# x rows loaded in other pieces, and a rank for each instruction in place of one for each stage

## The chip, the cores and the metric

The kernel runs on one core of a Trainium2 chip. A core has five engines with a queue of their own each: TensorE (PE) for matmuls, ScalarE (ACT), VectorE (DVE), GpSimd (POOL) and SyncE (SP, which here only issues DMAs). The metric is device time of one execution in microseconds; lower is better. The kernel before takes 227.81 us (median of three runs, 227.30 to 228.36).

## The reference

Two branches over a sequence of S = 2048 rows of D = 640, bf16, mixed by a gate that is computed from the same input:

```python
x = A_q
g = sigmoid((x * gate_w).sum(-1, keepdims=True))
a = A(x, A_k, A_v, A_shift_k, A_ssm_k, A_ssm_D)
b = B(x, B_w1, B_w2, B_w3, B_w4)
return g * a + (1 - g) * b
```

`A`: k is convolved with four taps per channel (`shift_k`) and multiplied by v, which gives `kv`; `kv` is convolved along the whole sequence with `ssm_k` (by FFT in the reference), `kv * ssm_D` is added, and the sum is multiplied by q (= x). `B`: layernorm of x, `@ w1`, gelu, the four column groups shifted by +1, -1, +2, -2 rows, `@ w2`, plus x; then layernorm, `@ w3` (to 1536), gelu, `@ w4`, plus the residual.

## The kernel before

**Tiling.** Sequence row s = 1024 c + 8 p + r lies on partition p; c is 0 or 1 and r, "row r" below, 0 to 7. So x is 16 tiles of 128x640, two halves (c) for each row r.

**The order is planned at build time.** The kernel's text creates 924 nodes (one instruction or a short run of matmuls each) with their tiles, a rough cost and a tag such as `xn:4`. `Prog._forward` then walks a model of the core: again and again it takes, over all engines, the node that can start earliest, and where several can start at the same time, the one with the highest priority. That fixes the order of every engine's queue, the PSUM pair (one of four) of every matmul job, and, in `assign_waits`, the semaphore waits. On the chip each engine then works through its list in that order; an instruction at the head of a list that waits holds all that stands behind it. `PRIO` gives one priority for each tag, so all nodes of a tag share it. The model's rate for plain loads is `RATE`, and `land` is what it adds from a load's last byte to its landing.

**The stages, by tag.**
- `x` loads (L709): pieces of rows as `X_LOADS` says, each piece as two DMAs (c = 0, 1); row 0 goes out on ACT's queue, all other pieces on SP's. The other loads follow on SP: `w1`, `k`, `v`, `kh` (the halo rows of k), `w2`, `FM` (transform tables), `ssm`, `D`, `gw`, `shk`.
- `fill`: 96 short matmuls on ones (L744) that need nothing; the planner puts them where TensorE would have nothing else, and drops those behind the last real matmul.
- First layernorm by `LN1_GROUPS` = (0), (1), (2,3), (4,5), (6,7): statistics on VectorE (`bn`, two for each half of a row and one aggregation, L874 and L876), for row 1 on ScalarE (`st`); an inverse root on GpSimd (`ln`, L854); the normalised row on VectorE (`xn`, L654); ten transposes (`xTp`, L913) and their eviction (`xTe`).
- `mm1` (L953, with `gelu1`), `tail` (GpSimd DMAs that shift the last columns), `gate` (L1010, four jobs of twenty one-column matmuls), `mm2` (L1061; `seed2` puts the residual into PSUM before, L1043; `x1` evicts, `sq` squares), second layernorm, `xT` (transposing DMAs), `mm3` (L1115, with `gelu3`), `mm4` (L1133, with `B`).
- `kv`, `kvb`: the four taps and the product with v, all on VectorE (L649), in four quarters `:0` to `:3`.
- The long convolution, for the two halves of the columns (half 0 and 1): transforms of the taps (`fwdh`) and of kv (`fwdk`), both L1164, evicted by ScalarE (`Sh`, `Sk`, L680); a unit for each half and parity, `:0` to `:3`, on VectorE: butterflies (`bh`, `bk`), `win`, `pw` with one accumulating DMA `pwa` on GpSimd's queue (L688), `pwz`, `fold`; the inverse transform `inv` (L1352; the last four rows `invl`, L1327), its eviction with the gate (`gy`, `gyl`), the product with q and the sum (`fin`, `finl`; in half 0 the sum is an accumulating DMA `fina`, L1378), the store `out`, `outl`.

`fwdk` needs all four quarters of kv. The inverse of half 0 needs units 0 and 1, that of half 1 units 2 and 3.

The nodes are numbered as they are created; the numbers are the same before and after the change.

Of the kernel before, what the change touches and what calls it, by code (L numbers as in the profile page):

```python
# [88 lines left out]
class Prog:  # L89
# [86 lines left out]
        node.land = land or (1.1 if final else 2.2)  # L176
        return node

    PRIO = {}

    def schedule(self):
        for n in self.nodes:
            n.base = frozenset(n.deps)
        for j in self.jobs:
            own = set(j.nodes)
            j.ext = [d for v in j.nodes if not v.first for d in v.base if d not in own]
            if j.seeded:
                j.nodes[0].soft = [d for v in j.pes for d in v.base if d not in own]
        for n in self.nodes:
            for d in n.deps:  # L190
                d.users.append(n)
        for n in self.nodes:
            n.prio = self.PRIO.get(n.tag, 0.0)
        self._forward()

    RATE = 400e3
    WINDOW = 3.4133
    PHASE = 2.4

    def _forward(self):  # L200
# [38 lines left out]
        while left:  # L239
# [59 lines left out]
            elif n.kind == "dma":  # L299
                link = max(link, xlink, t + 1.2) + n.bytes / self.RATE  # L300
                n.end = link + n.land
# [125 lines left out]
def _bf16_bits(a):  # L427
# [7 lines left out]
KV_DMA = ()  # L435
PW1 = (0, 1, 2, 3)
PW2 = ()
X_LOADS = ((0, 1), (1, 2), (2, 4), (4, 6), (6, 8))
LN1_GROUPS = ((0,), (1,), (2, 3), (4, 5), (6, 7))
SPLIT = (0,)  # L440
LN2_DVE = ()
# [7 lines left out]
XQ = {(0, 0): "act", (0, 1): "act"}  # L449
# [2 lines left out]
FIN1_DMA = 0  # L452
SEED2 = (0, 1, 2, 3, 4, 5, 6, 7)
SEED4 = (0, 1, 2, 3, 4, 5, 6, 7)
PRIO = {
# [36 lines left out]
}  # L492


def _freq(kap):
# [41 lines left out]
def bass_gated_mix__ssm_conv_h3__mixer_s_mlp__prompt_kernel(  # L537
    nc, A_q, A_k, A_v, A_shift_k, A_ssm_k, A_ssm_D, B_x, B_w1, B_w2, B_w3, B_w4, gate_w, out,
):
    D, F = 640, 1536  # L540
    P = Prog(nc)
# [17 lines left out]
    def V(o, n):  # L559
        return AR[:, o:o + n]  # L560
# [25 lines left out]
    X = V(oX, 10240).rearrange("p (c r d) -> p c r d", c=2, r=8)  # L586
# [3 lines left out]
    w1v = V(oW12, 3200).rearrange("p (c f) -> p c f", c=5)  # L590
    w1t = V(oW12 + 3200, 640).rearrange("p (c f) -> p c f", c=5)
# [6 lines left out]
    GM = V(oGM, 4096).rearrange("p (a i r s k) -> p a i r s k", a=2, i=2, r=4, s=2)  # L598
# [9 lines left out]
    ident = V(oID, 128)  # L608
# [82 lines left out]
    def load(queue, o, i, nbytes, tag="", **kw):  # L691
        return P.dma(queue, lambda e, ps: e.dma_start(o, i), w=[o], nbytes=nbytes, tag=tag, **kw)  # L692

    def dram(ap, offset, dims):
        return bass.AP(tensor=ap.tensor, offset=ap.offset + offset, ap=dims)

    def rows(t, c):
        return t[0, 1024 * c:1024 * c + 1024, :].rearrange("(p r) d -> p r d", r=8)
# [6 lines left out]

    for a, b in X_LOADS:
        P.stage = a
        for c in range(2):
            load(XQ.get((a, c), "sp"), X[:, c, a:b, :], rows(A_q, c)[:, a:b, :], 163840 * (b - a), tag="x", land=1.4 if b < 3 else 2.2)  # L709
    P.stage = ""  # L710
    load("pool", V(oID, 256).bitcast(U16), cI.ap(), 65536, tag="ident", cost=0.6)
    load("sp", w1v, B_w1.rearrange("(c p) f -> p c f", p=128), 890000, tag="w1")
    load("sp", SHKROW, dram(A_shift_k, 0, [[2560, 1], [1, 2560]]), 5120, tag="shk")
    w1s, w1d = w1v.rearrange("p c (g f) -> p c g f", g=4)[:, :, :, 128:160], w1t.rearrange("p c (g f) -> p c g f", g=4)
    P.op("pool", lambda e, ps: e.tensor_copy(w1d, w1s), r=[w1s], w=[w1d], cost=1.2, tag="w1t")
# [90 lines left out]
    for c in range(3):  # L806
        P.stage = c
        n = 128 if c < 2 else 64
# [6 lines left out]
              tag="tap")  # L815
# [13 lines left out]
    for a in range(2):  # L829
        P.stage = a  # L830
        o = TAP[:, 1, 8 * a:8 * a + 8, :]
        for d in (0, 128, 256):
            n = min(128, 320 - d)
# [131 lines left out]
    for sc in range(4):  # L965
# [10 lines left out]
        for j, d0 in enumerate(SHIFT):  # L976
# [4 lines left out]
            for carry, lst in todo.items():  # L981
                k0, rho0, n = lst[0][0], lst[0][1], len(lst)
# [21 lines left out]
    for g in range(4):  # L1004
        P.stage = g
        fns = []
        for i in range(4):
            rho, c = 2 * g + i // 2, i % 2
# [37 lines left out]
    for g in range(4):  # L1046
        P.stage = g
        for i in range(4):
            rho, c = 2 * g + i // 2, i % 2
# [3 lines left out]
            for hh in range(2):  # L1053
                for ft in range(5):
                    if ft < 4:
                        q = rho - SHIFT[ft]
# [27 lines left out]
        for rho in rhos:  # L1084
            for c in range(2):
                b = normal(rho, c, mean[:, rho, c:c + 1], RS2, NB2 if g in LN2_ACT else None)
# [21 lines left out]
    for sc in range(4):  # L1108
# [14 lines left out]
        for i in range(4):  # L1123
            rho, c = 2 * sc + i // 2, i % 2
# [275 lines left out]
    q1 = load_q(1, "s3")  # L1400
    inverse(1, "k0", "t1", q1, "s0")

    P.PRIO = PRIO
    P.schedule()
    P.assign_waits()
    with nc.Block() as block:  # L1406
# [29 lines left out]
```

## Time and profile before

| | us |
|---|---|
| median of three runs | 227.81 (227.30 to 228.36) |
| the profiled execution, its own time | 227.51 |
| its span, first to last instruction | 225.7 |
| DMA traffic | 34.05 MB |

| engine | busy us | share of the span |
|---|---|---|
| TensorE, matmuls | 217.8 | 97% |
| TensorE, weight loads | 139.0 | 62% |
| VectorE | 208.1 | 92% |
| ScalarE | 174.8 | 77% |
| GpSimd | 42.6 | 19% |

The granted TensorE clock is 1.00 throughout. How to read the views below: a row of the chain of waits, or of the timeline, has its start, its length, the engine and the line; "[0.48 <-DMA x]" says that the engine stood idle for 0.48 us before it and that a DMA of x ended that. "SPq" is SP issuing a DMA. Matmuls are pipelined, so the length of a single one (299 ns for 320 columns) is not its price; a run of them, divided by their number, is.

### The profile page before, as it was taken

Reading aid. Unit: us, or ns where it says so; the run is one execution under the profiler, and the core shown is the slowest. Engines: PE = TensorE matmul, PEld = TensorE weight load, DVE = VectorE, ACT = ScalarE, POOL = GpSimd, SP = SyncE. Lnnn points to the kernel's source line nnn. Section 1 sums busy time; section 2 is a strip of 40 time slices with the busy share of each in tenths; the row PEclk is TensorE's granted clock in tenths of the full one; section 3 lists DMA queues with packets and bytes.
Section 4 is the critical chain, followed back from the end, with each engine's and each line's share of the span. In section 5 each row is a group of like instructions: output and inputs, shape, how many; then the busy total and the mean of one; then the engine's idle time right before and its main releaser. Section 6 shows DMA issues by size and latency. Waiting matters only on the chain.

```text
span 225.7 us, 3992 instructions
## 1 busy us (share of the span) xinstructions
PE 217.8 (97%) x1575; PEld 139.0 (62%) x1587; DVE 208.1 (92%) x267; ACT 174.8 (77%) x292; POOL 42.6 (19%) x48
## 2 busy tenths in 40 slices
PE   6999999999999999999999999999999999999992
PEld 6695855557776664457754467754465566577771
DVE  4899999999999969999999999649999999999985
ACT  5889979879999999999785885594593465574392
POOL 1143654460004220203203200000010000332010
PEclk9999999999999999999999999999999999999999
DMA  6999997779823948061441680000077018488576
GB/s 166 392 401 402 334 348 251 151 143 243 281 96 84 310 85 341 7 116 33 87 86 30 108 130 0 3 0 0 0 132 219 0 35 200 58 174 110 126 135 215
DMA packets 36714, 34.05 MB, mean 151 GB/s; under 512 B 17508, under 2 KB 31719, under 8 KB 36568
## 3 DMA queue, kind: packets, MB, share of 16 engines
q1 hardware_dynamic: 31560, 23.97, 36.7%
q0 software_dynamic: 4848, 9.50, 19.2%
q10 hardware_dynamic: 288, 0.33, 0.5%
q8 instruction: 12, 0.20, 0.4%
q14 instruction: 6, 0.05, 0.1%
HBM read 21.47 MB, written 3.93 MB: 113 GB/s over the span
## 4 chain that ended last, share of the span: by engine, by line
PE 60%; DVE 24%; DMA 5%; issue 4%; ACT 4%; SPq 2%; DVEq 0%
PE PS L1133 23%; PE PS L1115 23%; DVE arena L649 20%; PE PS L1164 8%; PE PS L1352 6%; DMA arena<-in_A_q_dram 5%; ACT arena L680 3%; SPq L692 2%; DVE arena L874 2%; DVE arena L654 1%; PE PS L1061 1%; DVE arena L876 0%; ACT PS L1043 0%; DVE arena L1337 0%; DVEq L1406 0%
## 5 line engine op out<-in xcount | busy, mean ns | idle before, releaser
L649 DVE TENSOR_TENSOR arena<-arena 128x2560 bf16<-128x2560 bf16 (+5 forms) x175 | 185.9, 1120 | 10.4 <-ACT arena L680 8.9
L680 ACT ACTIVATE arena<-PS 128x640 bf16<-128x640 f32 (+6 forms) x142 | 104.9, 821 | 20.2 <-PE PS L1115 14.9
L1133 PE MATMUL PS<-arena 128*128 128x320 bf16 x384 | 54.0, 299 | 0.0
L1115 PE MATMUL PS<-arena 128*128 128x512 bf16 x232 | 51.4, 379 | 0.6 <-issue 0.2
L1133 PEld LDWEIGHTS PS<-arena 128*128 128x128 bf16 x384 | 37.4, 98 | 14.9 <-issue 0.3
L680 ACT ACTIVATE arena<-PS,arena 128x320 bf16<-128x320 f32 (+1 forms) x47 | 27.2, 616 | 22.5 <-PE PS L1133 20.2
L1115 PEld LDWEIGHTS PS<-arena 128*128 128x128 bf16 x240 | 23.3, 98 | 27.9 <-issue 0.3
L1164 PE MATMUL PS<-arena 128*128 128x320 bf16 x224 | 34.9, 300 | 0.7 <-DVE arena L649 0.4
L1164 PEld LDWEIGHTS PS<-arena 128*128 128x128 bf16 x224 | 20.6, 98 | 12.8 <-ACT arena L680 3.0
L666 ACT ACTIVATE arena<-arena 128x640 bf16<-128x640 bf16 (+2 forms) x34 | 25.9, 789 | 2.6 <-DVE arena L898 1.5
L1061 PE MATMUL PS<-arena 128*128 128x320 bf16 x160 | 23.4, 299 | 0.1
L953 PE MATMUL PS<-arena 128*128 128x512 bf16 (+1 forms) x121 | 22.8, 335 | 0.5 <-issue 0.2
L1043 ACT ACTIVATE PS<-arena 128x640 f32<-128x640 bf16 x32 | 22.6, 740 | 0.1
L854 POOL TENSOR_TENSOR arena<-arena 128x4 f32<-128x4 f32 (+1 forms) x9 | 12.9, 1441 | 39.3 <-DVE arena L654 33.2
L1061 PEld LDWEIGHTS PS<-arena 128*128 128x128 bf16 x160 | 15.2, 98 | 6.6 <-ACT PS L1043 0.7
L953 PEld LDWEIGHTS PS<-arena 128*128 128x128 bf16 x125 | 11.7, 98 | 8.5 <-DMA arena<-in_B_w_dram 0.3
L874 DVE BATCH_NORM_STATS2 arena<-arena 128x6 f32<-128x320 bf16 x28 | 12.1, 471 | 3.3 <-DMA arena<-in_A_q_dram 3.3
L688 POOL DMA_DIRECT2D arena<-arena x4 | 4.8, 1204 | 49.9 <-DVE arena L649 49.1
L1352 PE MATMUL PS<-arena 128*128 128x320 bf16 x96 | 13.7, 299 | 0.0
L1378 POOL DMA_DIRECT2D arena<-arena x4 | 5.1, 1275 | 42.5 <-DVE arena L649 40.4
L1352 PEld LDWEIGHTS PS<-arena 128*128 128x128 bf16 x96 | 9.3, 98 | 4.0 <-issue 0.2
L993 POOL DMA_DIRECT2D arena<-arena x18 | 10.1, 566 | 6.0 <-ACT arena L680 6.0
(42 smaller groups left out, 85.7 us busy)
## 6 DMA issues: line engine op xcount, KB each, us to landing
arena<-in_B_w_dram POOLq DMA_DIRECT2D x4, 960.0 KB, 7.9
arena<-in_A_k_dram SPq DMA_DIRECT2D x4, 640.0 KB, 13.7
arena<-in_A_v_dram SPq DMA_DIRECT2D x4, 640.0 KB, 14.8
arena<-arena POOLq DMA_DIRECT2D x4, 640.0 KB, 6.2
arena<-in_A_q_dram SPq DMA_DIRECT2D x4, 640.0 KB, 5.5
out_dram<-arena SPq DMA_DIRECT2D x15, 160.0 KB, 2.7
arena<-in_A_q_dram SPq DMA_DIRECT2D x6, 320.0 KB, 6.7
arena<-in_A_ssm_k_dram SPq DMA_DIRECT2D x3, 512.0 KB, 9.1
```

The costliest lines, as they stand in the source:

```text
L649: return dve(lambda e: e.tensor_tensor(o, a, b, op), [a, b], [o], c_tt(n), tag=tag, **kw)
L666: node = P.op("act", lambda e, ps: e.activation(o, i, func, **kw), r=r, w=[o], cost=c_act(n, naps, acc is not None, psum=False), tag=tag, ...
L680: node = P.op("act", lambda e, ps: e.activation(ov, inner(ps), func, **kw), r=r, w=[o], cost=c_act(n, len(r), acc is not None), job=job, t ...
L854: P.op("pool", lambda e, ps: e.tensor_tensor(r, v, hv, ALU.pow), r=[v, HALF], w=[r], cost=cost, tag="ln")
L874: dve(lambda e, o=o, x=x: e.bn_stats(o, x), [x], [o], 0.393, tag="bn", group=("bn", id(mv), rho, c))
L953: fns.append(lambda e, ps, b=b, c=c, lhsT=lhsT: e.matmul(bank(ps, b, 256 * n), lhsT, XT[:, c, r0:r0 + n, :], start=(c == 0), stop=(c == 4)))
L1043: P.seed(job, lambda e, ps: e.activation(two(ps, 320), x, ACTF.Copy), [X[:, c, rho, :]], c_act(640, psum=False), tag)
L1061: fns.append(lambda e, ps, hh=hh, ft=ft, lhsT=lhsT: e.matmul(bank(ps, hh, 320), lhsT, w2v[:, ft, 320 * hh:320 * hh + 320], start=False, st ...
L1115: fns.append(lambda e, ps, b=b, ft=ft, c=c, sc=sc: e.matmul(bank(ps, b, 512), w3h[ft // 6][:, c, 128 * (ft % 6):128 * (ft % 6) + 128], XT[ ...
L1133: fns.append(lambda e, ps, hh=hh, ft=ft, lhsT=lhsT: e.matmul(bank(ps, hh, 320), lhsT, w4h[ft // 6][:, ft % 6, 320 * hh:320 * hh + 320], st ...
L1164: fns.append(lambda e, ps, w=w, b=b, rhs=rhs, st=(first and n == 0), en=(n == len(ss) - 1): e.matmul(bank(ps, b, 320), w, rhs, start=st, s ...
L1352: fns.append(lambda e, ps, w=w, z=z, c=c, st=(n == 0), en=(n == len(terms) - 1): e.matmul(bank(ps, c, 320), w, z[:, c, :], start=st, stop=en))
```

## The change

1. **Pieces of x.** Rows (1,2), (3,4), (5,6) come as one piece each, rows 0 and 7 singly; before, rows 0 and 1 came singly and (2,3), (4,5), (6,7) as pieces. `LN1_GROUPS` stays as it was. There are five pieces, so ten DMAs, as before.
2. **Ranks.** `PRIO` by tag is replaced by `RANK`, a list with a number from 0 to 923 for each node, each number once; the node with the higher number goes first where both can start. No node ranks behind one that depends on it.
3. **The model's constants.** `RATE` 400e3 to 380e3, `land` of x 1.5, `w1` 850000 bytes and `land` 1.7.

No node is added or removed, and no tile, engine or queue of a node changes but for the pieces of x.

```diff
-            n.prio = self.PRIO.get(n.tag, 0.0)
+            n.prio = self.PRIO[n.idx]
...
-    RATE = 400e3
+    RATE = 380e3
...
-X_LOADS = ((0, 1), (1, 2), (2, 4), (4, 6), (6, 8))
+X_LOADS = ((0, 1), (1, 3), (3, 5), (5, 7), (7, 8))
...
-PRIO = {
-    "gyl:0a": 321, "finl:0a": 321, "outl:0a": 321, "gyl:0b": 320, "finl:0b": 320, "outl:0b": 320, "gyl:1a": 319,
...
+RANK = [
+    919, 921, 905, 922, 915, 906, 900, 860, 884, 842, 878, 787, 895, 918, 866, 923, 749, 811, 734, 850, 720, 716, 731,
...
+]
...
-            load(XQ.get((a, c), "sp"), X[:, c, a:b, :], rows(A_q, c)[:, a:b, :], 163840 * (b - a), tag="x", land=1.4 if b < 3 else 2.2)
+            load(XQ.get((a, c), "sp"), X[:, c, a:b, :], rows(A_q, c)[:, a:b, :], 163840 * (b - a), tag="x", land=1.5)
...
-    load("sp", w1v, B_w1.rearrange("(c p) f -> p c f", p=128), 890000, tag="w1")
+    load("sp", w1v, B_w1.rearrange("(c p) f -> p c f", p=128), 850000, tag="w1", land=1.7)
...
-    P.PRIO = PRIO
+    P.PRIO = RANK
```

What the list says, read node by node (position 0 is the highest rank; "c0", "c1" are the halves):

| | order before | order by rank |
|---|---|---|
| SP's first loads | x row 1 c0, c1; gw; x rows 2-3 c0, c1; shk; ssm 0; x rows 4-5 c0, c1; w1; ssm 1; x rows 6-7 c0, c1; FM 0, 1; k 1; k 0; v 3; D; w2 x8; ssm 2; v 2; k 3; v 0; k 2; kh; v 1 | shk; D; x rows 1-2 c0, c1; x row 7 c1; D; x rows 3-4 c1; x rows 5-6 c1; ssm 0; w1; x rows 3-4 c0; k 1; x rows 5-6 c0; w2 x2; v 2; k 0; FM 0; gw; x row 7 c0; FM 1; w2 x4; ssm 1, 2; w2 x2; k 3; v 0; k 2; v 3; v 1; kh |
| VectorE, rows of the first layernorm | row 0; half of row 2; `xn:0`; the rest by rows; `kv:0` begins behind `xn` of rows 4 and 5 | row 0; row 2; c1 of 3 and 4; `xn:0`; c1 of 6 and 5; `xn:1`; c1 of 7; c0 of 4 and 3; c0 of 6 and 5; `xn` of 2 to 5; one product of `kv:0`; c0 of 7 |
| TensorE around the first `fwdk` | all four `gate` jobs before it; then `fwdk` with two `mm2` jobs between | `gate:1`, `gate:2` and one `fwdh` right before it (positions 412 to 418), `fwdk` 606 at 420, `gate:3` at 425; two `mm2` jobs between |
| the first four jobs of `inv:0` | behind `fwdk:3` and the third `mm4:2` job | positions 676 to 710, before all four `mm4:1` jobs (722 to 742) |
| `fwdh`, `fwdk` of half 1 | 32 jobs, spread from before `mm3:0` to behind the third `mm4:2` job | eight among `mm3:0` and `mm4:0` (up to position 576), the other 24 in positions 629 to 709 |
| GpSimd's accumulating DMAs at the end | `fina`, `pwa:3`, `fina`, `fina`, `fina` | `fina`, `fina`, `pwa:3`, `fina`, `fina` |
| `fill` | 89 before the first `mm1`, seven at 70 to 81 us | 88 up to position 170 (the first `mm1` has 178), eight behind the last matmul of the work |

More of the change, by code (lines that the diff above doesn't have):

```diff
@@ L177, in dma @@
         return node
-    PRIO = {}
+    PRIO = ()
     def schedule(self):
@@ L454 @@
 SEED4 = (0, 1, 2, 3, 4, 5, 6, 7)
-PRIO = {
[36 rows of a table removed]
-}
+RANK = [
[40 rows of a table added]
+]
 def _freq(kap):
```

74 rows, old and new, of tables (PRIO, RANK) are left out of this document.

## The prediction

> **What bounds the kernel now.** I read the page's first part, then busy time in four stretches, then the chain of waits, then the weight loads of the long stretch, which are all recorded and so give the number of matmuls.
>
> ```profile
> span 225.7 us, 3992 instructions
> ...
> PE 217.8 (97%) x1575; PEld 139.0 (62%) x1587; DVE 208.1 (92%) x267; ACT 174.8 (77%) x292; POOL 42.6 (19%) x48
> ```
> ```profile
> 0.00:13.30 13.30, 11.39 (x134) 9.24 (x134) 9.18 (x39) 9.76 (x18) 3.20 (x8) 1.00 0.88 297
> 13.30:72.50 59.20, 58.32 (x508) 39.42 (x512) 58.10 (x67) 54.97 (x99) 19.62 (x27) 1.00 0.78 242
> 72.50:221.60 149.10, 148.12 (x934) 90.33 (x942) 139.25 (x160) 109.76 (x177) 19.80 (x14) 1.00 0.46 101
> 221.60:225.70 4.10, 0.00 (x0) 0.00 (x0) 1.53 (x6) 0.32 (x1) 0.00 (x0) 1.00 0.58 182
> ```
> ```profile
> 63.61 0.08 DVE arena L654
> ...
> 70.98 1.50 DVE arena L649
> ...
> 72.53 0.73 PE PS L1164 x4
> ...
> 86.00 10.74 PE PS L1115 x49
> ...
> 165.03 6.52 PE PS L1133 x48
> ...
> 221.73 0.46 DVE arena L1337
> 222.19 0.70 DVE arena L649 x3
> 222.89 0.23 DVEq L1406
> ```
> ```profile
> L1133 PEld LDWEIGHTS PS<-arena 128*128 128x128 bf16 x384 | 37.4, 98 | 14.9 <-issue 0.3 <-ACT PS L1043 0.2
> L1115 PEld LDWEIGHTS PS<-arena 128*128 128x128 bf16 x240 | 23.3, 98 | 27.9 <-issue 0.3 <-ACT arena L680 0.2
> L1164 PEld LDWEIGHTS PS<-arena 128*128 128x128 bf16 x168 | 15.3, 98 | 9.6 <-ACT arena L680 2.7 <-DVE arena L649 0.6
> L1352 PEld LDWEIGHTS PS<-arena 128*128 128x128 bf16 x96 | 9.3, 98 | 4.0 <-issue 0.2
> L1327 PEld LDWEIGHTS PS<-arena 128*128 128x128 bf16 x32 | 3.1, 98 | 1.2
> L1061 PEld LDWEIGHTS PS<-arena 128*128 128x128 bf16 x20 | 1.9, 98 | 1.1 <-ACT PS L1043 0.4
> ```
>
> The span is three terms. Up to 72.5 us VectorE is the chain: its last product of kv (the row at 70.98) ends, and the first `fwdk` starts at 72.53. From there TensorE carries it for 149.1 us. Then 4.1 us remain for the last eviction, the last sums and the last store. Is TensorE at its limit in the middle? A run of 512 columns goes at 10.74 / 49 = 0.219 us a matmul, one of 320 at 6.52 / 48 = 0.136. The six rows hold 240 of the first and 384+168+96+32+20 = 700 of the second kind: 52.6 + 95.1 = 147.7 us of 149.1. So no more than **1.4 us** is lost there. VectorE's waits in it, the last three of the next fence, are waits beside a full TensorE and worth almost nothing alone.
>
> ```profile
> 6.88 0.89 DVE L874 BATCH_NORM_STATS2 arena<-arena 128x6 f32<-128x320 bf16 x2 [0.79 <-DMA arena<-in_A_q_dram]
> ...
> 16.45 1.31 DVE L874 BATCH_NORM_STATS2 arena<-arena 128x6 f32<-128x320 bf16 x3 [0.48 <-DMA arena<-in_A_q_dram]
> ...
> 82.10 8.16 DVE L649 TENSOR_TENSOR arena<-arena 128x1280 bf16<-128x1280 bf16 x9 [1.92 <-ACT arena L680]
> ...
> 143.16 5.96 DVE L649 TENSOR_TENSOR arena<-arena 128x2560 bf16<-128x2560 bf16 x6 [2.48 <-ACT arena L680]
> ...
> 152.53 4.49 DVE L649 TENSOR_TENSOR arena<-arena 128x1280 bf16<-128x1280 bf16 x4 [3.41 <-ACT arena L680]
> ```
>
> Here a rule speaks for another reading. The Trainium skill (Perfetto Trace Analysis, Identifying the Most-Contended Engine) says that matmul busy time is no measure of TensorE's room and that the share of weight loading is; that share is 62% on the page, which would leave room. By the count of matmuls and their spacing there is none; what the rule would make of the time is the last rival.
>
> **Part 1: the pieces of x and SP's order (VectorE's term).** The change lets VectorE's two waits on x, 0.79 and 0.48 us, go, and makes others, since each engine takes its list in order. I take the landing by the number of KB that stand ahead and in the load. Rows for that:
>
> ```profile
> 2.48 0.43 SPq L692
> ...
> 6.12 10.31 DMA arena<-in_A_q_dram
> ```
> ```profile
> arena<-in_A_q_dram SPq DMA_DIRECT2D x1, 320.0 KB, 5.6
> ```
> ```profile
> 13.29 0.22 PEld L953 LDWEIGHTS PS<-arena 128*128 128x128 bf16 x3 [0.31 <-DMA arena<-in_B_w_dram]
> ```
> ```profile
> 21.11 0.52 PEld L766 LDWEIGHTS PS<-arena 128*128 128x128 bf16 x4 [0.58 <-DMA arena<-in_A_k_dram]
> ```
>
> Before, in SP's order: 960 KB (first half of rows 2-3) were there at 6.88, 1280 (second half) at 2.48 + 5.6 = 8.1, 3238 (w1) at 13.3, 4070 (first half of rows 6-7) at 16.4, 5926 (k 1) at 21.1. After, by straight lines between these: rows 1-2 second half, 966 KB: 6.9; rows 3-4 second half, 1446: 8.5; w1, 3078: 12.9; rows 3-4 first half, 3398: 13.9; rows 5-6 first half, 4358: 17.2; k 0, 5718: 20.6; row 7 first half, 6391: 22.3.
>
> ```profile
> 8.50 1.23 DVE L874 BATCH_NORM_STATS2 arena<-arena 128x6 f32<-128x320 bf16 x3
> 9.64 0.20 DVE L876 BATCH_NORM_AGGREGATE arena<-arena 128x2 f32<-128x12 f32 x1
> 9.75 0.84 DVE L874 BATCH_NORM_STATS2 arena<-arena 128x6 f32<-128x320 bf16 x2
> ...
> 26.02 1.51 DVE L654 TENSOR_SCALAR arena<-arena 128x640 bf16<-128x640 bf16 x4
> ```
>
> A statistic costs (9.64 - 8.50) / 3 = 0.38, an aggregation 0.11, so half a row 0.87; an `xn` 0.37. With row 0 done near 5.8 and the first half of row 2 near 6.7, VectorE waits 0.2 for the second half of rows 1-2, is through with it at 7.8 and waits 0.7 for rows 3-4. The five half rows, four `xn` and three small ones ranked next take 6.0, to 14.5: rows 3-4 first half has landed. Two half rows later, 16.3, it waits 0.9 for rows 5-6. Behind that everything has landed when its turn comes (k 0 at 20.6 against about 22, row 7 at 22.3 against about 23.5). Waits 1.8 in place of 1.27: **+0.5 us**. Three second-layernorm instructions of 0.08 (as at 63.61 in the chain) rank behind the last kv product now: **-0.2**. Ends: no wait at all, -1.27 - 0.2 = -1.5; each of the three waits as long as the longest of the two now, 2.4 against 1.27 less 0.2: +0.9. I take **+0.3**, the walk itself. If row 0's or row 2's half comes late, `st` on ScalarE, `ln:1` on GpSimd and the first `mm1` are late next; `mm1` has its own limit in w1, 0.4 us earlier than now.
>
> **Part 2: the ranks (TensorE's term).** No matmul comes or goes, so only what stands on which side of the first `fwdk` counts, and what is lost. One `gate` job moves behind it (+0.64, below); two fills go (-0.1). Two `mm2` jobs are behind it both before and after.
>
> ```profile
> 69.79 0.64 PE L1010 MATMUL PS<-arena 128*128 128x1 bf16 x20
> ```
>
> The loss is 1.4 us now; none would be -1.4. Above: 24 transform jobs of half 1 stand in one stretch, each with an eviction. Where they stand so now, the run is:
>
> ```profile
> 145.55 4.47 PE L1164 MATMUL PS<-arena 128*128 128x320 bf16 x30
> ...
> 146.44 6.06 ACT L680 ACTIVATE arena<-PS 128x640 bf16<-128x640 f32 x10
> 150.17 1.31 PE L1164 MATMUL PS<-arena 128*128 128x320 bf16 x8 [0.15 <-ACT arena L680]
> ```
>
> An eviction takes 6.06 / 10 = 0.61, a whole job 4 x 0.136 = 0.54, a half job 0.27; 38 matmuls, 5.2 us, took 5.9 (145.55 to 151.48), a loss of 0.8 for ten jobs. Uncovered, 24 jobs lose 1.9: +1.1 against now. In the new stretch four `mm3` jobs (2.2 each, one eviction) and four `inv:0` jobs (1.1) stand between, about 13 us of cover. I take a loss of 0.7, half of now's: -0.7, nearer the lower end because of that cover. Sum **-0.2**, ends -0.9 and +1.6.
>
> Moving `inv:0` forward moves `gy`, `fin`, two `fina` DMAs and loads of q too. `fin` fills VectorE's waits of 2.48 and 3.41; it costs nothing while TensorE is full, and 4 x 0.8 us if VectorE ever leads. SP passes no other load on its way there.
>
> **Part 3: the tail.** Now the last result goes straight to VectorE (0.46 + 0.70 + 0.23, the end of the chain). By rank the last is evicted by ScalarE, then two short VectorE instructions. About the same: **-0.1**, ends -0.5 and +0.5.
>
> Sum: +0.3 - 0.2 - 0.1 = 0.0 on a profiled execution of 227.5 (its span and 1.8 around it). The median of the runs is 0.3 above; I forecast **227.6, no change**, its own range 226.6 to 228.7. Under 0.5% (1.1 us) a measurement of this kernel can't tell from nothing.
>
> **Rivals.**
> - *The order works in full.* The loads of x land with no wait left and ScalarE keeps up in the stretch of transforms: -1.5 - 0.9 - 0.1 = -2.5, **225.1**; half of it, 226.3, is as likely. For it: the two waits exist and 147.7 of 149.1 shows that such packing is possible. Against: by the KB ahead, x comes later in the new order, not sooner.
> - *Slower: the transforms in one stretch wait on ScalarE.* ScalarE is at 0.61 for 0.54 or 0.27 of TensorE; all four PSUM pairs are then full and TensorE stands, with `mm3` and `mm4` behind it. Two such stretches (the first `fwdk`s, 16 evictions in positions 420 to 486, are as now) and late x: +0.9 + 1.6 - 0.1, **230.0**; with the stretch alone 229.2. It decides once the covers `mm3` and `inv` wait for a pair themselves.
> - *Slower, near the end: `pwa:3` queues behind two `fina`.* Accumulating DMAs land slowly:
> ```profile
> arena<-arena POOLq DMA_DIRECT2D x1, 640.0 KB, 6.0
> ```
>   VectorE has five 1.4 us instructions and one of 0.8 between `pwa:3` and its user, 7.8 us of cover for 6.0. With 320 KB twice right ahead (3 us each by this row) it lands after 12: +4, **231.8**. But four 0.8 and four 1.4 us VectorE instructions rank between the first `fina` and `pwa:3`, two of 1.4 behind the second; so rather one `fina`'s rest is ahead, some 1 to 2 us, and it decides only where `fina` itself, which waits for `B`, comes late.
> - *The list gives the same order where it matters*: 227.8. The list's order differs nearly everywhere, so this is small.
> - *By weight loads TensorE has room.* Then VectorE's waits of 1.92, 2.48 and 3.41 go: -7.8, 219.8. The skill's rule above is the one that says so; the matmul count speaks against it.
>
> **How the numbers follow.** Forecast 0.40 (0.32 within 0.5%, 0.05 below, 0.03 above). Order in full or by half 0.30, of that 0.28 faster. Transforms 0.18 and `pwa:3` 0.05, together 0.22 slower. Same order 0.05, same. Room 0.02, faster. So faster 0.35, same 0.40, slower 0.25. The range holds the forecast and most of the halves on both sides, 225.4 to 229.6.
>
> **What would show it.** VectorE's waits on x in the first 25 us: near 1.8 in all by my walk, none in the first rival. The start of the first `fwdk`: 72.5 plus 0.3. From there to TensorE's last matmul: 149.1 less 0.2. In the stretch of 24 transforms, idle TensorE that ScalarE ends. A wait of VectorE on an accumulating DMA near the end. I am wrong on the whole if the first `fwdk` moves by over 1 us, which would say that landing doesn't go by the KB ahead.

## The result, and the profile after

| | us | ratio to the kernel before, 95% interval |
|---|---|---|
| kernel before, beside the changed one | 227.97 (227.30 to 228.99, 7 runs) | |
| changed kernel | 230.46 (229.52 to 232.58, 7 runs) | 1.0112 (1.0069 to 1.0156) |
| changed kernel, measured again later | 231.28 (230.71 to 232.94, 6 runs) | 1.0134 (1.0091 to 1.0176) |

The change makes the kernel slower by a little over 1%; no change was forecast, and 229.6 was the upper end of the range. Executions of one and the same kernel differ by some 1.4 us with a short drop of the granted clock that some have and others don't (last section), so kernels are compared by their ratios, and traces with an eye on the clock.

The lines below are in the changed kernel's numbering, which is four higher than that of before (L649 is L653, L1133 is L1137, L1352 is L1356). An experiment's edit can shift them by a few more: L653 is L655 in experiment 1, L654 in 4, L656 in 6 and L658 in 7. The page's sum and the busy time by stretches (start:end, length, busy time of TensorE, its weight loads, VectorE, ScalarE and GpSimd, granted clock, DMA share, GB/s), with the same edges as before:

```profile
span 228.3 us, 3970 instructions
...
PE 218.0 (95%) x1565; PEld 139.3 (61%) x1579; DVE 207.9 (91%) x267; ACT 173.9 (76%) x292; POOL 43.3 (19%) x48
```
```profile
13.30:72.50 59.20, 57.59 (x490) 38.83 (x492) 56.26 (x60) 55.46 (x98) 20.75 (x26) 1.00 0.77 239
72.50:221.60 149.10, 146.12 (x936) 89.61 (x946) 137.77 (x155) 107.05 (x175) 19.46 (x14) 1.00 0.45 99
221.60:228.30 6.70, 2.21 (x17) 1.37 (x14) 3.72 (x15) 2.68 (x6) 0.00 (x0) 0.96 0.52 161
```

The busy times as a whole hardly moved (TensorE 218.0 for 217.8, VectorE 207.9 for 208.1): nothing became more work. In the long stretch TensorE lost 2.0 us of busy time (146.12 for 148.12), and what is missing there stands behind 221.60. So it waits somewhere. TensorE's timeline, first and last rows of what the prediction calls its term:

```profile
72.72 0.72 PE L1168 MATMUL PS<-arena 128*128 128x320 bf16 x4 [0.79 <-DVE arena L653]
```
```profile
200.12 13.20 PE L1137 MATMUL PS<-arena 128*128 128x320 bf16 x96
214.96 3.42 PE L1356 MATMUL PS<-arena 128*128 128x320 bf16 x24 [1.63 <-DVE arena L653]
...
219.84 3.97 PE L1331 MATMUL PS<-arena 128*128 128x320 bf16 x28
```

The same place in the kernel before:

```profile
206.18 6.68 PE L1133 MATMUL PS<-arena 128*128 128x320 bf16 x48
212.70 4.51 PE L1352 MATMUL PS<-arena 128*128 128x320 bf16 x32
217.05 4.51 PE L1327 MATMUL PS<-arena 128*128 128x320 bf16 x32
```

The span grew by 2.6 us. The first `fwdk` starts at 72.72 in place of 72.53: +0.2. From there to the end of the last matmul it is 223.81 - 72.72 = 151.1 us in place of 221.56 - 72.53 = 149.0: +2.1, of which 1.63 is one wait that the kernel before doesn't have: at 213 us the last inverse transforms (`inv:1`) wait for VectorE. The tail is 228.3 - 223.8 = 4.5 in place of 4.1.

Why is VectorE late? The chain of waits of the changed kernel, from where it leaves TensorE to where it comes back to it:

```profile
150.10 4.27 DMA arena<-in_A_q_dram
154.37 2.20 DVE arena L653 x3
...
156.86 8.58 DVE arena L653 x7
...
165.73 8.81 DMA arena<-arena
...
174.57 2.90 DVE arena L653 x2
...
212.51 2.31 DVE arena L653 x3
...
214.96 3.42 PE PS L1356 x24
```

In the chain before, TensorE and some evictions of ScalarE stood from 72.5 to 217 us, no VectorE and no DMA. Now two DMAs and some 50 us of VectorE stand in it. The first DMA, a load of q, cost nothing: VectorE's timeline shows no idle time before 154.37. The second is `pwa:2`, the accumulating DMA of unit 2: VectorE's next two instructions, `pwz:2`, wait for it, as its timeline shows (the work before ends at 157.60 + 11.49 = 169.1, then 5.47 us idle, which a DMA ends):

```profile
157.60 11.49 DVE L653 TENSOR_TENSOR arena<-arena 128x2560 bf16<-128x2560 bf16 x9
174.57 10.43 DVE L653 TENSOR_TENSOR arena<-arena 128x2560 bf16<-128x2560 bf16 x11 [5.47 <-DMA arena<-arena]
```

Unit 2's seven products (`pw:2`, 1.49 us each) show where that wait comes from. `pwa:2` adds the results of two of them. By stage priority these two came first and the other five behind them; by rank they come third and fifth, and only two products and one `fin:0` (0.8) are left behind the DMA's issue. GpSimd's timeline and the DMA issues between 155 and 184 us (KB each, us from issue to landing), before and after:

```profile
163.32 1.18 POOL L688 DMA_DIRECT2D arena<-arena  x1 [37.19 <-DVE arena L649]
```
```profile
arena<-arena POOLq DMA_DIRECT2D x1, 640.0 KB, 6.4
```
```profile
165.73 1.18 POOL L692 DMA_DIRECT2D arena<-arena  x1 [37.71 <-DVE arena L653]
```
```profile
arena<-in_A_q_dram SPq DMA_DIRECT2D x2, 640.0 KB, 7.1
arena<-arena POOLq DMA_DIRECT2D x1, 640.0 KB, 8.8
```

Before, VectorE had 6.7 us of work behind the issue (163.32 to 170.0, the end of the last of the five) for a DMA of 6.4. After, it has 3.4 (165.73 to 169.1), and the DMA takes 8.8, beside two loads of q of 640 KB that SP issues at 165.5 and 167.6. 8.8 - 3.4 = 5.4, the wait.

### The profile page after: what moved, and what is told of

Its sections match the earlier page's. It is cut to its first block, busy times and chain, and to the rows that moved or that the text cites. A ratio compares the mean times of both kernels' runs of the same rounds, so it can differ in the third digit from the quotient of the medians.

```text
span 228.3 us, 3970 instructions
## 1 busy us (share of the span) xinstructions
PE 218.0 (95%) x1565; PEld 139.3 (61%) x1579; DVE 207.9 (91%) x267; ACT 173.9 (76%) x292; POOL 43.3 (19%) x48
## 4 chain that ended last, share of the span: by engine, by line
DVE 45%; PE 30%; DMA 10%; ACT 6%; issue 3%; SPq 3%; POOL 2%; DVEq 0%
DVE arena L653 43%; PE PS L1119 14%; DMA arena<-in_A_q_dram 6%; PE PS L1168 6%; PE PS L1137 6%; ACT arena L684 5%; DMA arena<-arena 4%; PE PS L1356 3%; SPq L696 3%; DVE arena L658 2%; POOL arena L858 2%; DVE arena L878 1%; ACT PS L1047 1%; PE PS L1331 0%; DVE arena L880 0%
## 5 line engine op out<-in xcount | busy, mean ns | idle before, releaser
L653 DVE TENSOR_TENSOR arena<-arena 128x2560 bf16<-128x2560 bf16 (+6 forms) x175 | 186.1, 1119 | 12.1 <-DMA arena<-arena 5.5
L684 ACT ACTIVATE arena<-PS 128x640 bf16<-128x640 f32 (+5 forms) x142 | 105.0, 818 | 19.0 <-PE PS L1119 13.8
L1119 PE MATMUL PS<-arena 128*128 128x512 bf16 x231 | 52.3, 379 | 0.9 <-ACT arena L684 0.4
L1137 PE MATMUL PS<-arena 128*128 128x320 bf16 x384 | 53.0, 299 | 0.0
L1137 PEld LDWEIGHTS PS<-arena 128*128 128x128 bf16 x384 | 37.5, 98 | 15.1 <-issue 0.3
L1168 PE MATMUL PS<-arena 128*128 128x320 bf16 x224 | 34.6, 299 | 1.1 <-DVE arena L653 0.8
L1065 PE MATMUL PS<-arena 128*128 128x320 bf16 x160 | 22.7, 299 | 0.1
L858 POOL TENSOR_TENSOR arena<-arena 128x4 f32<-128x4 f32 (+1 forms) x9 | 13.9, 1547 | 31.1 <-DVE arena L658 28.8
L1356 PE MATMUL PS<-arena 128*128 128x320 bf16 x96 | 14.3, 299 | 1.6 <-DVE arena L653 1.6
L1356 PEld LDWEIGHTS PS<-arena 128*128 128x128 bf16 x96 | 9.2, 98 | 6.2 <-ACT arena L684 1.9
```

What stands on the lines that cost most here:

```text
L653: return dve(lambda e: e.tensor_tensor(o, a, b, op), [a, b], [o], c_tt(n), tag=tag, **kw)
L684: node = P.op("act", lambda e, ps: e.activation(ov, inner(ps), func, **kw), r=r, w=[o], cost=c_act(n, len(r), acc is not None), job=job, t ...
L858: P.op("pool", lambda e, ps: e.tensor_tensor(r, v, hv, ALU.pow), r=[v, HALF], w=[r], cost=cost, tag="ln")
L1065: fns.append(lambda e, ps, hh=hh, ft=ft, lhsT=lhsT: e.matmul(bank(ps, hh, 320), lhsT, w2v[:, ft, 320 * hh:320 * hh + 320], start=False, st ...
L1119: fns.append(lambda e, ps, b=b, ft=ft, c=c, sc=sc: e.matmul(bank(ps, b, 512), w3h[ft // 6][:, c, 128 * (ft % 6):128 * (ft % 6) + 128], XT[ ...
L1137: fns.append(lambda e, ps, hh=hh, ft=ft, lhsT=lhsT: e.matmul(bank(ps, hh, 320), lhsT, w4h[ft // 6][:, ft % 6, 320 * hh:320 * hh + 320], st ...
```

## The experiments

Theory A: this wait delays VectorE, VectorE's delay stops TensorE at 213 us, and that is the loss. Theory B: TensorE's lead covers the wait, and the time is lost in the stretch of 24 transforms fed by ScalarE, and in the late pieces of x.

**1. The two products first again.**
```diff
+for _n, _r in ((814, 188), (815, 187), (817, 184), (818, 182), (820, 179), (819, 173), (821, 171)):
+    RANK[_n] = _r
```


> Changed kernel, but the two products of unit 2 that its accumulating DMA adds together stand at the head of unit 2's products again, with five products behind them as cover. Theory A (the late accumulating DMA stops VectorE, VectorE's lag stops TensorE late): VectorE's wait of 5.47 us on that DMA falls below 1 us, the wait of TensorE of 1.6 us at the inverse transforms near 213 us goes, the last stretch goes from 4.5 to about 4.1 us, and the time falls by about 2.0 us, from 230.3 to some 228.3. Theory B (TensorE's lead covers that wait; the loss is in the stretch of transforms fed by ScalarE and in the late pieces of x): the wait goes and the time stays within 0.5 us of 230.3. First main transform at 72.7 us in both.

Measured: 228.17 us, ratio 1.0014 (0.9983 to 1.0046). VectorE's and TensorE's timelines, then the DMA issues:

```profile
200.64 9.50 DVE L655 TENSOR_TENSOR arena<-arena 128x2560 bf16<-128x2560 bf16 x9 [0.55 <-DMA arena<-arena]
215.03 2.01 DVE L655 TENSOR_TENSOR arena<-arena 128x640 bf16<-128x640 bf16 x4 [4.89 <-ACT arena L686]
```
```profile
212.67 3.42 PE L1358 MATMUL PS<-arena 128*128 128x320 bf16 x24
```
```profile
arena<-arena POOLq DMA_DIRECT2D x1, 640.0 KB, 5.7
```

The wait on `pwa:2` is gone, so is TensorE's, and the loss with them, as A said. (The 0.55 in the first row is a wait on `pwa:3`: with this edit one `fin:0` falls behind VectorE's `pwz:3`, and `pwa:3` goes ahead of a `fina`.) Issued 5 us earlier (160.4), `pwa:2` also lands at 166.1, hardly later than SP issues the first load of q (165.0), and takes 5.7 us. Two details were expected otherwise: the first `fwdk` starts at 72.23, not 72.7, though nothing ahead of it was changed, and the tail is 4.7 us (226.2 - 221.5), not 4.1. So 0.5 of the 2.1 us between the two profiles isn't the edit's; from the first `fwdk` to the last matmul it is 149.3 us in place of 151.1, -1.8. Note the second row: VectorE now stands idle for 4.89 us near the end, where the kernel before has 1.07. The new order had made VectorE early, and the wait had eaten that.

**2. The order of every engine as changed, but the loads of q wait until `pwa:2` has landed.**
```diff
+    P.nodes[862].deps.add(P.nodes[816])
+    P.nodes[863].deps.add(P.nodes[816])
```


> Changed kernel, with the order of all engines kept; only the two loads of q of the next half (640 KB each), which ran beside the accumulating DMA of unit 2, now wait until that DMA has landed. Theory A with the DMA slowed by its neighbours: it lands after about 5.7 instead of 8.8 us, VectorE waits about 2.4 instead of 5.5 us for it, TensorE's wait at 213 us shrinks from 1.6 us to under 0.3, and the time falls by 1.4 to 2.0 us. If the DMA is long for another reason than its neighbours: it still takes 8 us or more, the wait stays at 5 us, and the time stays at 230.3. Theory B: the wait shrinks and the time stays.

Measured: 229.04 us, ratio 1.0025 (0.9996 to 1.0055).

```profile
172.56 11.83 DVE L653 TENSOR_TENSOR arena<-arena 128x2560 bf16<-128x2560 bf16 x12 [2.25 <-DMA arena<-arena]
```
```profile
214.44 3.42 PE L1356 MATMUL PS<-arena 128*128 128x320 bf16 x24
```
```profile
arena<-arena POOLq DMA_DIRECT2D x1, 640.0 KB, 5.6
```

With no load beside it, the same DMA takes 5.6 us. VectorE waits 2.25, and TensorE no longer waits at all. The order of every engine is the changed kernel's, so the thin cover alone is free; it takes the company of the loads as well to exceed VectorE's lead. (The company alone, 8.8 us against the old cover of 6.7, would make a wait of 2.1, which by this run is free too under the new ranks; that wasn't tried.) The rule of the Trainium skill (DMA: Bandwidth & Descriptors, Issuing engines are not separate DMA queues) that DMAs of all engines run on the same 16 DMA engines and interleave agrees with this pair, 5.6 alone and 8.8 in company.

**3. The late pair alone, in the kernel before.**
```diff
-            n.prio = self.PRIO.get(n.tag, 0.0)
+            n.prio = self.PRIO.get(n.tag, 0.0) - (0.5 if n.idx in (814, 815) else 0.0)
```


> Kernel before, but the two products that unit 2's accumulating DMA adds come behind the other five products of the unit, as the changed kernel has it; nothing else of the change. Theory A: VectorE waits 3 to 6 us on that DMA, and the time rises by 0.5 to 2 us over the kernel before, that is to 228.4 to 229.9. Theory B: the wait appears and the time stays at 227.9.

Measured: 234.78 us, ratio 1.0286 (1.0241 to 1.0332): the right direction, three times the size. Only VectorE's list differs from the kernel before. In it the pair now comes third and fourth of the seven products, with three behind it and not none as the expectation says, and two `fin:0` and a product of unit 3 move by a few places. VectorE, TensorE, and the stretches around TensorE's wait:

```profile
177.81 6.69 DVE L649 TENSOR_TENSOR arena<-arena 128x2560 bf16<-128x2560 bf16 x7 [5.78 <-DMA arena<-arena]
```
```profile
219.51 6.09 PE L1352 MATMUL PS<-arena 128*128 128x320 bf16 x32 [4.76 <-DVE arena L649]
```
```profile
214.70:219.50 4.80, 0.05 (x1) 0.00 (x0) 4.77 (x6) 0.79 (x1) 1.26 (x1) 0.98 0.77 166
219.50:225.60 6.10, 6.09 (x34) 3.86 (x35) 4.20 (x8) 2.84 (x6) 0.00 (x0) 0.73 0.22 43
```

Nearly the same wait of VectorE (5.78 for 5.47) costs TensorE 4.76 us here and 1.63 in the changed kernel. And behind the 4.76 the mean granted clock is 0.73 for 6 us: the 32 matmuls that took 4.51 take 6.09. The span of this profile is 8.3 us longer than before (234.0 for 225.7): 4.76 + 1.58, and 1.9 that aren't the edit's, a later first `fwdk`:

```profile
74.42 2.08 PE L1164 MATMUL PS<-arena 128*128 128x320 bf16 x14 [0.42 <-DVE arena L649]
```

Up to there every engine has the order of the kernel before; the mean granted clock was 0.67 from 10.0 to 13.3 us and 0.91 from there to 20. The profiled execution took 235.80 us, 1.0 more than the median, so the 6.2 us between the medians (234.78 against 228.56 beside it) are no check on the sum of 4.76 and 1.58. What the expectation had not counted is that the kernel before has almost no lead of VectorE at this place.

**4. The half of x that VectorE waits for, earlier.**
```diff
+RANK[9], RANK[19] = RANK[19], RANK[9]
```


> Changed kernel, with the load of the first half of x rows 5 and 6 issued ahead of the load of k that stood before it. All theories: VectorE's wait for x at 16.8 us (1.18 us) falls to under 0.3 us, and the first main transform goes from 72.7 us to 71.6 to 72.0. Theory A (VectorE's lag near 174 us sets the end): the late wait stays at about 5 us, TensorE's wait at 213 us takes back what was won early or part of it, and the time falls by 0 to 1.1 us. Theory B (early x is a main part of the loss): the time falls by a full 1.0 us or more.

Measured: 228.71 us, ratio 1.0023 (0.9995 to 1.0051).

```profile
72.26 0.72 PE L1169 MATMUL PS<-arena 128*128 128x320 bf16 x4 [0.15 <-DVE arena L654]
```
```profile
173.68 10.42 DVE L654 TENSOR_TENSOR arena<-arena 128x2560 bf16<-128x2560 bf16 x11 [5.09 <-DMA arena<-arena]
```
```profile
214.05 3.42 PE L1357 MATMUL PS<-arena 128*128 128x320 bf16 x24 [1.18 <-DVE arena L654]
```

One `mm1` job and one `fill` change places with the edit. VectorE's wait of 1.18 us for rows 5 and 6 is gone (waits on x of 0.82 and 0.45 us stand at 4.8 and 8.3 us instead), the first `fwdk` comes 0.46 us earlier, and the late wait is still there. How much of the 0.46 the edit gave can't be read from this pair. Experiment 1 has the changed kernel's loads and orders up to the first `fwdk`, and there the same wait was short and the first `fwdk` as early:

```profile
16.25 1.28 DVE L880 BATCH_NORM_STATS2 arena<-arena 128x6 f32<-128x320 bf16 x3 [0.26 <-DMA arena<-in_A_q_dram]
```
```profile
72.23 0.72 PE L1170 MATMUL PS<-arena 128*128 128x320 bf16 x4 [0.57 <-DVE arena L655]
```

The rows explain at most 0.9 of the time (0.46 earlier, and 1.18 in place of 1.63 at 213 us). By ratio it is 2 us, over the 1.1 that theory A allowed and as theory B said, and the profiled span is 1.7 us shorter, 0.8 of it behind the last matmul (226.6 - 222.9 = 3.7 us). That rest was not traced to the edit; 3.7 to 4.7 us is what this tail takes in the profiled executions shown here, with the same instructions in it. So this run alone decides nothing between the theories.

**5. The changed kernel again**, beside the next three, since experiment 4 came back further than its trace says.

> The changed kernel itself once more, beside the kernel before on the same chip, as the measure for the other three runs of this call. If the runs with one part undone came back to the kernel before because of their edits, the ratio here is 1.008 to 1.015 as in its first measurement, VectorE again waits some 5 us on unit 2's accumulating DMA and TensorE 1.2 to 1.8 us at 213 us. If they came back because the first measurement of the changed kernel lay high, the ratio here is 1.002 to 1.006.

Measured: ratio 1.0134 (1.0091 to 1.0176). The loss is real, and in this profiled execution larger, for a reason that can be read:

```profile
175.75 40.97 DVE L653 TENSOR_TENSOR arena<-arena 128x2560 bf16<-128x2560 bf16 x39 [6.76 <-DMA arena<-arena]
```
```profile
216.13 3.42 PE L1356 MATMUL PS<-arena 128*128 128x320 bf16 x24 [2.93 <-DVE arena L653]
```

The DMA took 10.1 us, 1.3 longer than in the first profile, VectorE waited 1.3 longer, and TensorE 1.3 longer: 2.93, where 1.2 to 1.8 was expected.

**6. Both repairs together** (the edits of 1 and 4).

> Changed kernel with both repairs: unit 2's two products ahead of its other five, and the first half of x rows 5 and 6 ahead of the load of k. Theory A: no wait of VectorE above 1 us on a DMA after 155 us, no wait of TensorE at 213 us, first main transform at about 72.0 us (the early repair is worth 0.5 us at that place, as it was alone), and since no late wait takes the early gain back it reaches the end: 0.2 to 0.7 us under the run with the first repair alone, ratio to the kernel before 0.996 to 1.000. If the early gain is lost again on the way (ScalarE in the stretch of transforms), the ratio is 1.000 to 1.003.

Measured: 227.90 us, ratio 0.9976 (0.9947 to 1.0005). `pwa:2` takes 5.7 us, TensorE has no late wait, VectorE a late one of 0.56 us on `pwa:3`, and the first `fwdk` is at 72.13:

```profile
72.13 0.72 PE L1171 MATMUL PS<-arena 128*128 128x320 bf16 x4 [0.41 <-DVE arena L656]
```

That is clearly faster than the changed kernel; against the kernel before, the interval just reaches 1. That the earlier x adds anything to experiment 1 is not shown: the first `fwdk` is 0.1 us earlier than there, and the two intervals overlap.

**7. And a product of kv moved towards the wait for GpSimd at 30.7 us.**
```diff
+for _n, _p in ((156, 260), (279, 261), (280, 264), (275, 266), (347, 267), (276, 268)):
+    RANK[_n] = 923 - _p
```


> As the run before it, and besides four products of kv and two evictions stand ahead of the last normalised row of x, so that VectorE has work while GpSimd computes the scale of row 6 (a wait of 1.00 us at 30.7 us in the changed kernel and in all runs from it). Theory A: that wait falls to under 0.3 us, the first main transform comes at 71.0 to 71.5 us, and the time is 0.7 to 1.2 us below that of the run with two repairs: ratio to the kernel before 0.991 to 0.997, faster than both kernels. If something other than VectorE's products sets the first main transform, it stays at 72 us and the ratio equals that of the run with two repairs.

Only one of the six nodes moved, 156, is a product of kv, so less was tried than the expectation says. Measured: 228.00 us, ratio 0.9990 (0.9965 to 1.0015), a miss. VectorE, with TensorE's row for `mm1` behind it, and the latter in the run before:

```profile
30.10 0.45 DVE L663 TENSOR_SCALAR arena<-arena 128x640 bf16<-128x640 bf16 x1 [1.00 <-POOL arena L863]
30.46 1.49 DVE L658 TENSOR_TENSOR arena<-arena 128x2560 bf16<-128x2560 bf16 x1
```
```profile
45.61 1.67 PE L962 MATMUL PS<-arena 128*128 128x512 bf16 x7 [0.17 <-issue]
```
```profile
44.79 2.10 PE L960 MATMUL PS<-arena 128*128 128x512 bf16 x9 [0.17 <-issue]
```

The product came one instruction too late: behind the row that waits, not ahead of it, so the wait of 1.00 stayed. The other normalised rows came later for it, and TensorE with them, by 0.8 us. TensorE reaches the first `fwdk` without a wait there, and no earlier: in this run TensorE was as late at 72 us as VectorE.

**8. The new ranks with the old pieces of x.**
```diff
-X_LOADS = ((0, 1), (1, 3), (3, 5), (5, 7), (7, 8))
+X_LOADS = ((0, 1), (1, 2), (2, 4), (4, 6), (6, 8))
```


> Changed kernel with the old pieces of x (rows 0 and 1 singly, then 2 to 7 in pairs) under the new ranks: the ranks without the other part of the change. Theory A (the ranks carry the loss, at unit 2's products): the late wait of VectorE on the accumulating DMA stays at 4 us or more, TensorE's wait at 213 us stays within 0.6 us of the changed kernel's, VectorE's waits on x in the first 20 us change by less than 1 us, and the ratio is 1.006 to 1.016. Theory B (the pieces carry it): the first main transform comes by 1 us or more earlier than 72.7 us and the ratio is 1.004 or less.

Measured: 230.72 us, ratio 1.0116 (1.0069 to 1.0163).

```profile
75.21 3.12 PE L1168 MATMUL PS<-arena 128*128 128x320 bf16 x11 [0.64 <-DVE arena L653]
```
```profile
177.46 40.96 DVE L653 TENSOR_TENSOR arena<-arena 128x2560 bf16<-128x2560 bf16 x39 [4.80 <-DMA arena<-arena]
```
```profile
217.83 3.42 PE L1356 MATMUL PS<-arena 128*128 128x320 bf16 x24 [0.97 <-DVE arena L653]
```

The late wait of VectorE stays with the new ranks and constants alone, so the new pieces don't cause it; TensorE's is 0.97, 0.66 below the changed kernel's, where theory A allowed 0.6. The time is the same, but not made up of the same parts. With the old pieces under these ranks the first `fwdk` comes 2.5 us later, not earlier. From there to the end of the last matmul it is 226.7 - 75.2 = 151.5 us, of which some 1.7 go to a mean granted clock of 0.83 from 75.2 to 85 us, in this execution; 149.8 without them, 1.3 less than in the changed kernel, and the tail is 3.7, 0.8 less. So this run says that the late wait comes with the ranks, and doesn't split the loss between the two parts of the change. The new pieces alone, under the old stage priorities, weren't tried: the planner then lays out nearly the whole kernel anew, and the comparison would be of two other orders.

**All traces together.** Us, from the rows above and those of the same views:

| kernel | `pwa:2`, issue to landing | VectorE's wait for it | TensorE's wait at `inv:1` | difference |
|---|---|---|---|---|
| 1 and 6, pair first | 5.7 | none | none | |
| 2, loads of q later | 5.6 | 2.25 | none | |
| 8, old pieces | 8.1 | 4.80 | 0.97 | 3.83 |
| 4, x earlier | 8.4 | 5.09 | 1.18 | 3.91 |
| changed kernel | 8.8 | 5.47 | 1.63 | 3.84 |
| changed kernel again | 10.1 | 6.76 | 2.93 | 3.83 |
| 3, kernel before with the late pair | 9.8 | 5.78 | 4.76 | 1.02 |

Under the new ranks VectorE leads TensorE by 3.8 us at this place: a wait below that costs nothing (row 2), and every microsecond above it one microsecond. In the kernel before, as far as the one run of experiment 3 shows, the lead is 1.0. So the ranks did win something, 2.8 us of lead on an engine that isn't the bound, where it doesn't show in the time.

## Why the prediction was wrong

**VectorE's term, +0.3:** right in its number, in part by luck. The first `fwdk` moved by +0.2 in this pair of profiles; in three more with the same order up to there (experiments 1, 2 and 5) it stands at 72.23, 72.72 and 72.59, for 72.53 before. Of the three waits on x in the walk, 0.2, 0.7 and 0.9, the first was 0.28 at 6.47 us, the second wasn't there, and the third was 1.18:

```profile
16.77 1.28 DVE L878 BATCH_NORM_STATS2 arena<-arena 128x6 f32<-128x320 bf16 x3 [1.18 <-DMA arena<-in_A_q_dram]
...
30.69 1.16 DVE L658 TENSOR_SCALAR arena<-arena 128x640 bf16<-128x640 bf16 x3 [1.00 <-POOL arena L858]
```

That is 1.46 in all for 1.8, and the third wait is 0.26 to 1.19 in the four profiles. So landing by the KB ahead held to half a microsecond or so (16.8 for 17.2), not finer. Not foreseen were the wait for GpSimd of 1.00 us at 30.7, and an earlier start (first statistic at 3.19 in place of 3.76) that paid part of it.

**TensorE's term, -0.2:** this failed, by 2.2 us. Not in what the step worked out: with the late wait repaired (experiment 1), the stretch from the first `fwdk` at 72.23 to the end of the last matmul takes 149.3 us, so the jobs and the transforms in one stretch are worth about +0.3, well within the ends of -0.9 and +1.6. (The `gate` job in it was priced at the length of its row, 0.64; by the start of what follows, 73.27 to 73.77, it cost 0.50.) The step that failed is its last one, that `fin`, and with it what moves on VectorE, "costs nothing while TensorE is full". That sentence priced VectorE's moved work, not the order inside it. For the accumulating DMAs it looked at one of the four, `pwa:3`, counted its cover and put a rival there; `pwa:2`, whose cover the same list halves, was not counted: its wait of 5.47 us cost TensorE 1.63, and 2.93 in experiment 5. And it took no lead of VectorE over TensorE at `inv:1`, the one figure that says from when a wait of VectorE is not free.

**The tail, -0.1:** 4.5 for 4.1 in the two profiles, but 3.7 to 4.7 among kernels that share its instructions; nothing can be told from it.

**The rivals.** "Slower, `pwa:3` behind two `fina`" had the right kind of cause in the wrong unit: with a chance of 0.05, a price of +4 and no wait there in the trace after. "The transforms in one stretch wait on ScalarE" fell: in that stretch the changed kernel shows one wait,

```profile
136.88 2.11 PE L1119 MATMUL PS<-arena 128*128 128x512 bf16 x9 [0.38 <-ACT arena L684]
```

and experiments 1 and 2 took the loss away with that stretch as it was. "The order works in full" fell as well: even with both repairs the ratio is 0.9976 (0.9947 to 1.0005), not the 0.989 of 225.1. "TensorE has room" fell: in experiment 1 VectorE had 4.89 us to spare near the end, and TensorE's stretch still took 149.3 us. (The prediction read the rule for this rival by half: the section of the Trainium skill that it names, Perfetto Trace Analysis, Identifying the Most-Contended Engine, has MFU, the share of the peak rate of matmuls, beside the share of weight loading.) "The list gives the same order where it matters" fell with `pwa:2`.

## What to carry to other kernels

When an order changes, list every DMA that a computing engine later waits for, and for each count the work that stands between its issue and the wait, before and after, and the transfers that are issued beside it; one left out is enough. For an engine that isn't the bound, work out its lead at the places where the bound waits for it: below that lead its waits are free, above it they cost one for one. A reordering can win lead and lose time in the same list. Lead is not time: here, with the one bad place mended, the ratio was 0.9976 (0.9947 to 1.0005).

## What the hardware showed that was not expected

**The granted clock drops for a few microseconds behind short stalls, in some executions only.** The same four matmuls of the first `fwdk`, behind a stall of 0.79 us in the changed kernel (72.72 in the section on the result) and of 0.92 in experiment 2, with the stretch behind them in that run:

```profile
72.72 1.25 PE L1168 MATMUL PS<-arena 128*128 128x320 bf16 x4 [0.92 <-DVE arena L653]
```
```profile
72.00:76.00 4.00, 3.28 (x31) 2.13 (x32) 3.96 (x7) 2.31 (x5) 2.20 (x1) 0.59 0.92 342
```

At a mean clock of 0.59 they take 1.25 us for 0.72, and the four microseconds cost about 1.6. The changed kernel measured again stalled 2.93 us at 213 us and ran on undisturbed (24 matmuls in 3.42); experiment 3, with 4.76, ran at 0.73. The Trainium skill (TensorE: Matmul & The Clock Gate, What's actually happening) has the clock fall after an idle window of some 3.4 us. Experiment 3 agrees; a drop behind a stall of 0.92 us does not by the stall alone. Ahead of it stand 45 matmuls of one column (69.57 to 71.1 us) and four of 320; whether the 45 count as idle was not tried, and they stand there in the changed kernel too, where no drop followed.

**A GpSimd power of four elements a partition takes 1.01, 1.16 or 2.25 us**, here the shortest and the longest in the changed kernel:

```profile
15.49 1.01 POOL L858 TENSOR_TENSOR arena<-arena 128x4 f32<-128x4 f32 x1 [2.54 <-DVE arena L658]
...
28.32 2.25 POOL L858 TENSOR_TENSOR arena<-arena 128x4 f32<-128x4 f32 x1 [5.83 <-DVE arena L658]
```

The long one ran beside a VectorE product of two tiles (128x2560, from 28.19 to 29.7), and VectorE then waited 1.00 us for it. The Trainium skill (SBUF — State Buffer, Who interferes with whom) says that a VectorE instruction with two SBUF inputs contends with GpSimd's reads; the two durations agree, but no run took the product away from there.
